# Windowed attention and max-out feed-forward: columns in the order 8 to 255, 0 to 7, 256 to 259

## The chip, the cores and the metric

The kernel runs on one core of a Trainium2 chip. The metric is the time of the device in microseconds. Three runs of the kernel before took 408.97, 409.05 and 409.37 us; the median is 409.05 us. A profile of one execution is read besides: it lists each instruction of the five engines (PE, the matrix engine; DVE, the vector engine; ACT, the scalar engine; POOL and SP, which here mostly issue transfers) and each transfer between memory and the on-chip buffers.

## The reference: what is computed

There are 8 sequences of 4160 positions with 192 features in 8 heads of 24. Each position and head has 7 logits. Their softmax weighs the position itself and the six before it (zeros ahead of a sequence's start). The result goes through a feed-forward layer with two first matrices, of which the larger product is taken element by element.

```python
w = weight_gen - np.max(weight_gen, axis=-1, keepdims=True)
w = np.exp(w)
w = w / (np.sum(w, axis=-1, keepdims=True) + 1e-09)
x_pad = np.concatenate([np.zeros((B, pad, D)), x], axis=1)      # pad = 6
x_unf = x_pad[:, idx, :].reshape(B, S, K, H, group)             # 7 taps
out = np.einsum('bshk,bskhg->bshg', w, x_unf).reshape(B * S, D)
h1 = out @ w1
h2 = out @ w2
return np.maximum(h1, h2) @ w_out                               # 192 -> 1024 -> 192
```

Input and output are 32-bit floats. The kernel computes in bfloat16 behind the softmax.

## The kernel before, in words

**Layout.** The 33280 positions are laid on 128 partitions of 260 consecutive positions each; sixteen partitions hold one sequence. A "column" is one position on every partition. Columns are worked in batches of 16 (the seventeenth has 4). The window of the first six columns of a partition reaches into the end of the partition before; that is the halo. It is masked to zero on the partitions that begin a sequence (`msk`).

**Softmax.** For each batch, ACT takes exp of the logits (`exp_sum`), DVE sums seven taps (`red`), ACT takes the logarithm (`ln`), DVE subtracts it from the logits (`shift`), and ACT takes exp again (`weights`), writing each weight twice in bfloat16. No maximum is subtracted.

**Attention.** DVE multiplies 7 shifted windows of x with the weights (`mul`) and adds them up in three steps (`adds`). In the first two batches (`mul` in pieces of 4 columns) PE does the sum together with the transposition, by matmuls with an identity (`sum_transpose`), and ACT copies the result to `yt`. Later a transposing transfer on SP's queue does it (`transpose`), in units of 8 columns.

**Feed-forward.** Since max(h1, h2) = h1 + relu(h2 - h1), PE multiplies with the difference of the two first matrices (`wd`), ACT takes the relu from the accumulators into `rd`, and PE adds up relu times `wo` and the attention's result times `w10`, the product of the first matrix and `wo`, made once at the start. ACT evicts the output (`evac`), SP stores it. Hidden tiles are worked in groups of two, later three; `hidden` writes each group's order on PE and ACT by hand, and `softmax_steps` and `extra` place the softmax and attention of later batches between them by a table of due times.

**The order around the change.** The program is issued in a written order; every engine works its own list in order. At the start, SP issues the first logits (`load_wg(0, ...)`, L520), the halo in two transfers (L523), the first four x columns (L537), then the rows of the first matrices (`ws`, L541 and L549), the next four x columns, the second halves of these rows, and the second logits. Each of SP's transfers uses one of eight semaphores in turn, so the ninth waits until the first has landed. POOL issues later x and logits. PE runs matmuls without use (`keep_warm`) until the first product is there. `w_diff` builds `wd` on DVE and copies parts across partition halves. At the end `rest_of_results` does the last outputs, and SP waits for all stores.

The lines that carry this are few:

```python
for step in (exp_sum, red, ln, shift):
    for i in range(2):
        step(0, i, 2)
...
first_mul = mul(0, 0)
...
keep_warm(30)
w_diff(0, nc.scalar.copy)
```

Of the kernel before, what the change touches and what calls it, by code (L numbers as in the profile page):

```python
# [9 lines left out]
FP32 = mybir.dt.float32  # L10
# [13 lines left out]
def kernel(  # L24
# [20 lines left out]
    RPB = P // B  # L45
    G = D // H
# [29 lines left out]
    pwg = ctx.enter_context(tc.tile_pool(name="pwg", bufs=4))  # L76
    pxb = ctx.enter_context(tc.tile_pool(name="pxb", bufs=2))
    pe_ = ctx.enter_context(tc.tile_pool(name="pe", bufs=2))
    psm = ctx.enter_context(tc.tile_pool(name="psm", bufs=3))
    pm = ctx.enter_context(tc.tile_pool(name="pm", bufs=1))  # L80
    pen = ctx.enter_context(tc.tile_pool(name="pen", bufs=2))
    py = ctx.enter_context(tc.tile_pool(name="py", bufs=2))
    pyt = ctx.enter_context(tc.tile_pool(name="pyt", bufs=6))
    prd = ctx.enter_context(tc.tile_pool(name="prd", bufs=7))
    first_ps = ctx.enter_context(ExitStack())
# [3 lines left out]
    def later_ps():  # L89

        first_ps.close()
        for k in ("ab", "c", "r"):
            ps[k] = ctx.enter_context(tc.tile_pool(name="pps_" + k, bufs=1, space=bass.MemoryType.PSUM))
# [7 lines left out]
    def load_wg(b, eng):  # L101
        c0, n = BATCHES[b]
        wg_ts[b] = pwg.tile([P, n * WGC], FP32, name="wg_t", tag="wg")
        return eng.dma_start(
            out=wg_ts[b],
            in_=bass.AP(tensor=weight_gen.tensor, offset=c0 * WGC,
                        ap=[[CPP * WGC, P], [1, n * WGC]]),
        )

    def load_x(b, o, n, halo=True):  # L110

        if b not in xb_ts:
            xb_ts[b] = pxb.tile([P, (16 + PAD) * D], BF16, name="xb_t", tag="xb")
        load = nc.gpsimd.dma_start(  # L114
            out=xb_ts[b][:, (PAD + o) * D:(PAD + o + n) * D],
            in_=bass.AP(tensor=x.tensor, offset=(BATCHES[b][0] + o) * D,
                        ap=[[CPP * D, P], [1, n * D]]),
        )
        if b > 0 and o == 0 and halo:
            load_halo(b)  # L120
        return load

    def load_halo(b):

        if b not in xb_ts:
            xb_ts[b] = pxb.tile([P, (16 + PAD) * D], BF16, name="xb_t", tag="xb")
        nc.gpsimd.dma_start(out=xb_ts[b][:, 0:PAD * D],
# [708 lines left out]
```

## Time and profile before

| what | value |
|---|---|
| median of three runs | 409.05 us (408.97 to 409.37) |
| profiled execution, first to last instruction | 408.4 us |
| PE busy | 398.9 us (98%) |
| DVE busy | 371.7 us (91%) |
| ACT busy | 357.1 us (87%) |
| POOL busy | 72.5 us (18%) |
| granted PE clock | 1.000 |
| HBM read, written | 35.96 MB, 25.56 MB |
| first multiply of x and weights on DVE | 9.75 us |
| first hidden matmul on PE | 16.10 us |
| first output matmul on PE | 28.99 us |
| end of DVE's last attention sum | 378.5 us |
| issue of the last stores | 405.38 us |

The profiled execution's own time is its span of 408.4 us, and the runs' median lies 0.65 us above it; the difference is what lies around the first and last instruction. The body is read as a rhythm: PE works three hidden tiles and the outputs that belong to them in about 4.3 us, and ACT's relus and evictions stand in the gaps. A row of the timeline gives the start, the duration, the engine, the line in the code, the operation, what is written and read, and the shapes; in brackets stands the idle time of the engine just before and what ended it.

### The profile page before, as it was taken

What the parts mean: (1) busy time and instruction counts of PE and PEld (TensorE: products, weight loads), DVE (VectorE), ACT (ScalarE), POOL (GpSimd) and SP (SyncE); (2) the same over time, 40 slices, a digit from 0 to 9 for tenths busy, and PEclk for the clock granted to TensorE, in tenths of its full rate; (3) what the DMA queues carried; (4) which work ended last, traced back from release to release, by engine and by line L of the source; (5) the groups of instructions that cost most, each with busy time, mean ns of one, the idle gap of its engine ahead of it and who ended that gap; (6) DMA issues with size and microseconds to landing.
All of it is one profiled execution on the core that took longest, in us unless ns stands there. A gap on an engine that the chain in (4) does not pass through costs nothing.

```text
span 408.4 us, 16153 instructions
## 1 busy us (share of the span) xinstructions
PE 398.9 (98%) x7422; PEld 317.6 (78%) x7422; DVE 371.7 (91%) x216; ACT 357.1 (87%) x424; POOL 72.5 (18%) x101
## 2 busy tenths in 40 slices
PE   7899999999999999999999999999999999999996
PEld 2589989777777777777877777777778777777796
DVE  4999999999999999999999999999999999999000
ACT  6799899999899998898998999998999988988872
POOL 0311012212222112121211122220122220210000
PEclk9999999999999999999999999999999999999999
DMA  8958399767658674976786588478648647654514
GB/s 242 218 125 219 75 186 167 168 165 173 147 113 237 151 167 105 244 201 69 234 203 84 123 248 202 65 243 180 128 109 239 169 68 237 154 127 111 145 55 142
DMA packets 62785, 65.70 MB, mean 161 GB/s; under 512 B 47711, under 2 KB 51679, under 8 KB 62718
## 3 DMA queue, kind: packets, MB, share of 16 engines
q1 hardware_dynamic: 54334, 40.54, 36.7%
q0 software_dynamic: 8240, 24.04, 29.9%
q8 instruction: 58, 0.95, 1.0%
q10 hardware_dynamic: 144, 0.10, 0.1%
q14 instruction: 9, 0.07, 0.1%
HBM read 35.96 MB, written 25.56 MB: 151 GB/s over the span
## 4 chain that ended last, share of the span: by engine, by line
PE 91%; ACT 4%; DMA 3%; issue 1%; SPq 0%; DVE 0%; ACTq 0%
PE op_ps L339 41%; PE hd L299 39%; PE op_ps L351 8%; DMA xs<-in_x_dram 3%; ACT rd_t L309 2%; PE hdp L299 1%; PE yps L248 1%; ACT yt L255 1%; ACT w1t L675 0%; ACT e_t L135 0%; ACT en_t L167 0%; DVE xb_t L620 0%; ACT wd L591 0%; ACT w L668 0%; ACT w1T L633 0%
## 5 line engine op out<-in xcount | busy, mean ns | idle before, releaser
L309 ACT ACTIVATE rd_t<-hd 128x1024 bf16<-128x1024 f32 (+1 forms) x206 | 234.7, 1187 | 27.5 <-PE hd L299 26.3
L339 PE MATMUL op_ps<-wo,rd_t 64*128 64x192 bf16 x4160 | 211.4, 243 | 0.1
L339 PEld LDWEIGHTS <-rd_t 64*128 64x128 bf16 x4160 | 181.7, 94 | 15.7 <-ACTq L372 0.3
L299 PE MATMUL hd<-yt,wd 64*128 64x512 bf16 (+1 forms) x1584 | 188.1, 360 | 0.7 <-issue 0.6
L182 DVE TENSOR_TENSOR m_t<-xb_t,en_t 128x10752 bf16<-128x10752 bf16 (+1 forms) x37 | 187.4, 5070 | 0.2
L299 PEld LDWEIGHTS <-wd 64*128 64x128 bf16 x1776 | 94.5, 94 | 43.2 <-issue 2.8
L224 POOL CAST gate<-yt 128x1 f32<-128x1 bf16 x29 | 37.8, 1305 | 264.3 <-DMA yt<-y_t 264.3
L198 DVE TENSOR_TENSOR m_t<-m_t 128x4608 bf16<-128x4608 bf16 (+1 forms) x30 | 74.1, 2470 | 0.1
L395 ACT COPY o_t<-op_ps 128x384 f32<-128x384 f32 (+1 forms) x99 | 57.3, 589 | 12.8 <-PE op_ps L339 12.8
L351 PE MATMUL op_ps<-w,yt 64*128 64x192 bf16 x780 | 56.0, 243 | 0.4 <-ACT w L668 0.4
L351 PEld LDWEIGHTS <-yt 64*128 64x128 bf16 x780 | 38.6, 94 | 16.7 <-issue 1.3
L204 DVE TENSOR_TENSOR m_t<-m_t 128x3072 bf16<-128x3072 bf16 (+1 forms) x29 | 50.0, 1723 | 0.1
L167 ACT ACTIVATE en_t<-wg_t 128x896 bf16<-128x896 f32 (+2 forms) x45 | 35.8, 821 | 0.0
L207 DVE TENSOR_TENSOR y_t<-m_t 128x1536 bf16<-128x1536 bf16 (+1 forms) x29 | 27.3, 941 | 0.5
L114 POOL DMA_DIRECT2D xb_t<-in_x_dram x33 | 17.6, 534 | 32.0 <-ACT rd_t L309 19.8
L147 DVE TENSOR_REDUCE sum_t<-e_t 128x64 f32<-128x448 f32 (+2 forms) x31 | 19.6, 635 | 3.3 <-ACT e_t L135 3.3
L156 DVE TENSOR_TENSOR wg_t<-wg_t,sum_t 128x280 f32<-128x280 f32 (+5 forms) x46 | 22.0, 481 | 0.0
L135 ACT ACTIVATE e_t<-wg_t 128x896 f32<-128x896 f32 (+2 forms) x18 | 16.1, 901 | 2.6 <-DMA wg_t<-in_weight_gen_dram 2.6
L309 ACT ACTIVATE rd_t<-hdp 128x1024 bf16<-128x1024 f32 x16 | 16.3, 1056 | 0.5 <-PE hdp L299 0.4
L299 PE MATMUL hdp<-yt,wd 64*128 64x256 bf16 x192 | 13.2, 270 | 0.7 <-issue 0.5
L615 PE MATMUL warm<-ident 128*128 128x512 bf16 x38 | 10.7, 449 | 2.6 <-DVE ident L562 2.6
L248 PEld LDWEIGHTS <-m_t 64*128 64x128 bf16 x636 | 10.1, 95 | 2.6 <-DVE m_t L182 2.5
(45 smaller groups left out, 65.9 us busy)
## 6 DMA issues: line engine op xcount, KB each, us to landing
out_dram<-o_t SPq DMA_DIRECT2D x22, 768.0 KB, 4.8
xb_t<-in_x_dram POOLq DMA_DIRECT2D x30, 384.0 KB, 5.2
out_dram<-o_t SPq DMA_DIRECT2D x20, 384.0 KB, 3.1
wg_t<-in_weight_gen_dram POOLq DMA_DIRECT2D x14, 448.0 KB, 5.3
xb_t<-xb_t POOLq DMA_DIRECT2D x16, 288.0 KB, 5.4
wg_t<-in_weight_gen_dram SPq DMA_DIRECT2D x2, 448.0 KB, 4.4
xs<-in_x_dram SPq DMA_DIRECT2D x2, 384.0 KB, 7.2
xb_t<-in_x_dram POOLq DMA_DIRECT2D x3, 192.0 KB, 4.4
```

The lines of the kernel that those rows point to most:

```text
L156: nc.vector.tensor_tensor(out=w_t, in0=w_t, in1=_sub(s_ts[b], hs.start, [[1, hs.stop - hs.start], [0, K]]), op=ALU.subtract)
L167: nc.scalar.activation(out=_sub(en_ts[b], (o * WGC + j * N * K) * 2, [[2 * N, K], [2, N], [1, 2]]), in_=_sub(wg_ts[b], (o * H + j * N) * K ...
L182: return nc.vector.tensor_tensor(out=m_out, in0=x_in, in1=_sub(en_ts[b], o * WGC * 2, [[2, K * n * H], [0, G // 2], [1, 2]]), op=ALU.mult,)
L198: nc.vector.tensor_tensor(out=taps(0, 1, 3), in0=taps(0, 1, 3), in1=taps(3, 1, 3), op=ALU.add)
L204: nc.vector.tensor_tensor(out=taps(0, 2, 2), in0=taps(0, 2, 2), in1=taps(1, 5, 2), op=ALU.add)
L207: nc.vector.tensor_tensor(out=_sub(y_ts[b], o * D, [[64, 2], [P, 3 * w // 2], [1, 64]]), in0=taps(0, 1, 1), in1=taps(2, 1, 1), op=ALU.add,)
L224: nc.gpsimd.tensor_copy(out=gate, in_=yt[:, 0:1])
L299: nc.tensor.matmul(hid_out(t, f, j), lhsT=wd_at(j, s, f // 4, f % 4 * P, P), rhs=_sub(yt_ts[u][half(j), :], (s + j) % 3 * P, [[3 * P, w // ...
L309: relu_of[t0] = nc.scalar.activation(out=rd[:, k * 1024:(k + n) * 1024], in_=hd[:, at:at + n * 1024], func=AF.Relu)
L339: return nc.tensor.matmul(op_out(c), lhsT=rd[half(r), k * 1024 + at:k * 1024 + at + P], rhs=wo[half(r), f * D:(f + 1) * D], start=False, s ...
L351: nc.tensor.matmul(op_out(c + j), lhsT=yt_ts[u][half(j), (3 * i + (s + j) % 3) * P:(3 * i + (s + j) % 3 + 1) * P], rhs=w10[half(j), s * D: ...
L395: nc.scalar.copy(out=_sub(o, c % 24 * D, [[D, len(qs)], [h * D, 2], [1, D]]), in_=_sub(tile_, at + (qs[0] - p) * D, [[D, len(qs)], [512, 2 ...
```

## The change: what it does

- **Order of columns.** The columns are worked in the order 8 to 255, 0 to 7, 256 to 259. `actual` maps the place in the order to the column, for loads and stores. The first batch is now columns 8 to 23; its halo, columns 2 to 7, lies on the same partition and needs no mask. Columns 0 to 7 stand in the batch before the last; their x goes to a tile of its own (`"wrap"`), with a halo from the partition before, loaded on POOL's queue after a memset of one row, and masked by one ACT instruction (`wrap_mask`) shortly before use.
- **Start.** The first logits are loaded in two halves; the second half goes on SP's queue after the weight rows' last 64 rows. The halo and the first four columns come in one transfer each. The second four columns come by POOL's queue, as bfloat16 and behind the first exp. Only the first half of the first softmax is done ahead of the first multiply; the second half stands after the first hidden tiles. `ident` is built ahead of the mask. Two of the three copies of the first `w_diff` move from ACT to DVE. The w1E copy of the second half moves behind the second half's weights. `keep_warm` has 24 and 4 matmuls instead of 30 and 8.
- **Sums.** The sums of the softmax are kept for the whole kernel in two tiles (`s_first`, `s_rest`), and the logarithm is written to a tile of its own.
- **Guard.** At the end (`sums_in_range`) DVE takes the largest and smallest sum, compares them with 1e18 and 1e-18, a transfer brings the 128 results into one row, and one integer is made of them. Every engine loads it into a register. If it is not zero, a loop over 260 columns computes everything again with the maximum subtracted (`with_maximum`); otherwise the engines branch past it.

The diff, cut to its core:

```diff
+    def actual(v):
+        return v + 8 if v < LAST - 8 else v - (LAST - 8) if v < LAST else v
...
+        key, at = (b, o) if c < LAST - 8 else ("wrap", 0) if c < LAST else (NB - 2, 8)
...
+        if "wrap" in xb_ts and t is xb_ts["wrap"]:
+            nc.gpsimd.memset(t[0:1, 0:PAD * D], 0.0)
+            nc.gpsimd.dma_start(
+                out=t[1:P, 0:PAD * D],
+                in_=bass.AP(tensor=x.tensor, offset=(CPP - PAD) * D, ap=[[CPP * D, P - 1], [1, PAD * D]]),
+            )
...
+    def wrap_mask():
+        halo = xb_ts["wrap"][:, 0:PAD * D]
+        nc.scalar.activation(out=halo, in_=halo, func=AF.Copy, scale=msk[:, 0:1])
...
-        load_wg(0, nc.sync)
-        nc.vector.memset(xs[0:1, 0:PAD * D], 0.0)
-        for p0, p1 in ((1, 16), (16, P)):
+        xb_ts[0] = pxb.tile([P, (16 + PAD) * D], BF16, name="xb_t", tag="xb")
+        load_wg(0, nc.sync, 0, 8)
+        for at, c, n in ((0, 2, PAD), (PAD, 8, 4)):
             nc.sync.dma_start(
...
         load_w(0)
-        load_first(4)
+        load_w_rest()
+        load_wg(0, nc.sync, 8, 8)
         load_w(1)
         load_wg(1, nc.sync)
...
-        for step in (exp_sum, red, ln, shift):
-            for i in range(2):
-                step(0, i, 2)
+        first_exp = exp_sum(0, 0, 2)
+        for step in (red, ln, shift):
+            step(0, 0, 2)
...
-        for o in (0, 4, 8, 12):
-            weights(0, o)
+        weights(0, 0)
+        weights(0, 4)
+        for at, n in ((0, PAD), (PAD, 4)):
+            nc.vector.tensor_copy(out=xb_ts[0][:, at * D:(at + n) * D], in_=xs[:, at * D:(at + n) * D])
...
-        keep_warm(30)
-        w_diff(0, nc.scalar.copy)
-        nc.vector.tensor_copy(out=xb_ts[0][:, (PAD + 4) * D:(PAD + 8) * D], in_=xs[:, (PAD + 4) * D:])
+        keep_warm(24)
+        w_diff(0, (nc.scalar.copy, nc.vector.tensor_copy, nc.vector.tensor_copy))
+        behind(first_exp, load_x(0, 4, 4))
         behind(first_mul, load_x(0, 8, 4))
...
-        keep_warm(8)
+        keep_warm(4)
         mul(0, 4)
+        exp_sum(0, 1, 2)
         nc.scalar.copy(out=w1["T"], in_=ws["T", 0])
-        nc.scalar.copy(out=w1["E"][:, HF:F], in_=ws["E", 0][:, HF:F])
...
-        w_diff(1, nc.vector.tensor_copy)
-        sum_transpose(1)
+        w_diff(1, (nc.vector.tensor_copy,) * 3, lambda: red(0, 1, 2))
+        sum_transpose(1, ahead=lambda: ln(0, 1, 2))
+        shift(0, 1, 2)
         red(1)
+        weights(0, 8)
         mul(0, 8)
+        weights(0, 12)
+        nc.scalar.copy(out=w1["E"][:, HF:F], in_=ws["E", 0][:, HF:F])
         hidden(1)
...
+        if s == 4 and b == NB - 3:
+            wrap_mask()
...
+    sums_in_range()
     rest_of_results(OUTS[-1])
+    work.close()
+    again = nc.values_load(odd_any, min_val=0, max_val=1, ...)
+    with tc.If(again != 0, preferred_fallthrough_block=False):
+        with_maximum()
```

and of the new functions at the end:

```python
def sums_in_range():
    for i, (op, test, bound) in enumerate(((ALU.max, ALU.is_gt, SUMS[1]), (ALU.min, ALU.is_lt, SUMS[0]))):
        for j, s_t in enumerate(s_parts):
            at = 2 * i + j
            nc.vector.tensor_reduce(out=odd[:, at:at + 1], in_=s_t, op=op, axis=AX.X)
            nc.vector.tensor_single_scalar(out=odd[:, at + 4:at + 5], in_=odd[:, at:at + 1], scalar=bound, op=test)
    nc.vector.tensor_reduce(out=odd[:, 8:9], in_=odd[:, 4:8], op=ALU.max, axis=AX.X)
    nc.gpsimd.dma_start(out=odd_row, in_=odd[:, 8:9])
    nc.vector.tensor_reduce(out=odd[0:1, 9:10], in_=odd_row, op=ALU.max, axis=AX.X)
    nc.vector.tensor_copy(out=odd_any, in_=odd[0:1, 9:10])
```

## The prediction

> **What bounds the kernel now.** I read the busy line and the chain on the page first, then the waits of TensorE (PE), then the timeline of the first 35 us and of the last 10. The page, parts 1 and 4:
>
> ```profile
> PE 398.9 (98%) x7422; PEld 317.6 (78%) x7422; DVE 371.7 (91%) x216; ACT 357.1 (87%) x424; POOL 72.5 (18%) x101
> ...
> PE 91%; ACT 4%; DMA 3%; issue 1%; SPq 0%; DVE 0%; ACTq 0%
> ```
>
> The body is PE's: the table of 10 us windows gives PE 10.00 of 10 from 60 us to 400 us. So only what moves PE's start, what stalls it, and what follows its last matmul can move the end. PE's waits show the start:
>
> ```profile
> PE warm L615 <- DVE ident L562: 2.6, 1, 2.6
> PE yps L248 <- DVE m_t L182: 1.3, 1, 1.3
> ...
> PE op_ps L351 <- ACT w L668: 0.4, 1, 0.4
> ```
>
> The third is the last real wait: the first output matmul (28.99 us) waits for ScalarE's (ACT's) copies of w10. From there PE runs on. The timeline shows what leads there:
>
> ```profile
> 9.08 0.56 DVE L574 CAST xb_t<-xs 128x768 bf16<-128x768 f32 x1 [1.40 <-DMA xs<-in_x_dram]
> 9.75 2.96 DVE L182 TENSOR_TENSOR m_t<-xb_t,en_t 128x5376 bf16<-128x5376 bf16 x1
> ...
> 12.77 1.40 PE L248 MATMUL yps<-ident,m_t 64*128 64x64 bf16 x84 [1.29 <-DVE m_t L182]
> ...
> 13.34 0.62 ACT L586 COPY wd<-wd 64x512 bf16<-64x512 bf16 x1 [2.48 <-DVE wd L584]
> ...
> 15.26 0.80 ACT L255 CAST yt<-yps 128x768 bf16<-128x768 f32 x1
> ...
> 28.30 0.64 ACT L668 CAST w<-pw 64x192 bf16<-64x192 f32 x2
> ...
> 28.99 0.42 PE L351 MATMUL op_ps<-w,yt 64*128 64x192 bf16 x6 [0.35 <-ACT w L668]
> ```
>
> VectorE (DVE) idles 1.40 us until the first x columns land at 9.06, multiplies from 9.75 (call this start X), PE transposes, and from 15.26 ACT works without a gap to 28.94. That is the start's critical path: the x transfer, the first multiply, then ACT.
>
> **Part 1: when the first multiply starts.** The transfers ahead of it shrink from 448+67.5+504+384 = 1403 KB to 224+576+384 = 1184 KB. 219 KB at the first slice's 242 GB/s are 0.9 us: landing 8.15, if the rest stays. Two things do not. In the packet records one 3072-byte packet of this transfer took 1.84 us (median 0.17), and 14 of its 16 shares had landed by 7.4: without such a straggler the new landing would be near 6.4. And the second x columns, formerly SyncE's (SP's) after the weight rows, are now issued by POOL right after the first exp. That exp can end near 4.2 (half a logit load, 0.52 for the half exp); POOL's first packet came 1.37 after its issue at 13.02, so packets flow from 5.6, beside the end of the transfer we wait for. The same 192 KB piece needed 0.97 us alone (16.45 to 17.42 in the middle shares), so SP's is delayed by up to 0.97; I take 0.7, what of it lies before the landing. Bounds: 7.05 (no straggler) and 8.85 (the same one); no row tells which, so I take the middle, 8.0. With 0.58 for the cast and 0.11 to the next start, X = 8.7 (7.75 to 9.55) instead of 9.75. The cast of the six halo columns (1152 elements, 0.84 by L574's rate), which replaces the masked copies L568 and L570, runs while the later transfer flows: free; without that cover 0.84.
>
> The Trainium skill, "DMA: Bandwidth & Descriptors", section "Queues, rings and completion order", has each DMA engine take turns between queues, a packet of some nine or more rows at a time. By that rule POOL's eight rows pass in one turn, and the landing would be 8.3 instead of 8.0. The trace has both queues moving at once from 14.4 to 16.4 us, but does not show the turns.
>
> **Part 2: from X to the w10 copies.** Before, ACT's first `yt` copy waited behind three `wd` copies and began at X+5.51. Now two of those are DVE's, and the copy starts when PE is done: 2.96 + 0.05 + 1.40 + 0.05 = X+4.46. A gain of 1.05. But the half of the first softmax that ran under the transfer wait now stands in ACT's and DVE's gapless stretch. DVE from X, by start-to-start times: multiply 2.88, two differences 0.60 and 0.75, two copies 0.60, multiply 2.88, difference 0.72, half reduction 0.53, three copies 0.87, half shift 0.57: done at X+10.40. The cast L620 (0.72) is gone. ACT: `yt` 0.69, half exp 0.45, copy 0.52, relu 0.92, exp 0.84, relu 0.90 end at X+8.85; the half ln waits for the half reduction (X+9.0); the second `yt` ends at X+9.98; the four weight exps wait for the shift: X+10.43. Then 4 x 0.30, the w1E copy 0.52, two relus 1.82, ln 0.19, two relus 1.81, w1t 1.37, two exps 0.60, `yt` 0.68, relu 0.91, w10 copies 1.13: end X+20.66. Before: 28.94 = X+19.19. So the stretch is 1.47 longer and break-even is at X = 8.28. With X = 8.7, PE's body starts 0.42 later; bounds -0.53 and +1.27. DVE's own path (its third multiply ends at X+14.31 instead of X+13.37) gives -0.1 and is covered by ACT's. The T rows of the weights pass the same DMA engines: 384 KB more ahead and 219 less put them near 11 to 12.7 against the need at X+3.48 = 12.2: even; a lateness there adds one to one.
>
> The early `ident` (the 1.02 us memset L521 leaves DVE) and the 24+4 instead of 30+8 warm matmuls change only filler: PE's gap before the transposes grows from 1.3 to about 2.5 us. If that gap cost PE its clock (the first warm matmuls stand 0.43 apart, later ones 0.21), transposes and first hidden tiles (2.9 us) would double; the page grants full clock in all slices, and I cost it at nothing.
>
> **Part 3: the body.** Sums go to long-lived tiles and ln to a new one: same instructions, no new wait. Storing columns elsewhere costs nothing; the stores are the same size. Two logit loads instead of one for batch 15: 0.55 of POOL, which idles 9 us before its next gate. New is the mask of the late halo: POOL memset and a 127-row transfer, then one ACT instruction of 1152 elements in group 78, about 352 us:
>
> ```profile
> 351.68 0.26 ACT L151 ACTIVATE sum_t<-sum_t 128x32 f32<-128x32 f32 x1
> 351.86 1.02 ACT L309 ACTIVATE rd_t<-hd 128x1024 bf16<-128x1024 f32 x1
> 353.18 0.80 ACT L395 COPY o_t<-op_ps 128x768 f32<-128x768 f32 x1 [0.30 <-PE op_ps L339]
> 354.53 2.86 ACT L309 ACTIVATE rd_t<-hd 128x1024 bf16<-128x1024 f32 x3 [0.56 <-PE hd L299]
> ```
>
> By L570 (864 elements, 1.02) it takes 1.35. It stands between the short ln and the relu; the relu slips by 1.35, ACT's idle 0.30 takes some, the eviction is 1.05 late. PE needs that PSUM tile after two hidden tiles, 0.45 after the eviction ended: a stall of 0.6. The halo transfer, issued near 347 behind POOL's load (345.38) and memset, lands in 3 to 5 us, in time or up to 1 late in the same place. Low bound 0 (if the eviction's real slack is larger), high 1.5; I take 0.6.
>
> **Part 4: the end.** The check of the sums is 11 DVE instructions and a POOL transfer after DVE's last sum at 378.5: four reductions over 384 or 1696 values (1.08 for 896 read, L147) make about 5 us, the transfer 4; done by 390, under PE's tail. If it were not, every engine's end would wait. After the last store each engine now loads a register from SBUF, compares, and branches over the rarely run block; SP also passes four more waits.
>
> ```profile
> 404.87 0.48 ACT L383 COPY o_last<-op_ps 128x384 f32<-128x384 f32 x1
> 405.38 0.34 SPq L386 DMA_DIRECT2D out_dram<-o_last  x1
> ```
>
> SP's last issue ends at 405.72, its 13 closing waits take 0.065 each, yet it finishes them at 407.49, as the last store lands at 407.4: 0.9 slack. Added: four waits 0.26, branch steps 0.16, and the register load. No row shows one: at least a wait (0.06), at most a round trip like the last store's (1.8). I take 1.0, as it moves one word but must go to SBUF and back. 1.42 - 0.9 = 0.5 late. The jump may need instructions not fetched yet: the page's instruction queue moved 58 packets of 16 KB, median 0.98 us, at most 1.76. Zero or one such, I take 0.3 for it: tail +0.8 (0 to 2.9).
>
> **The sum.** 0.4 + 0.6 + 0.8 = +1.8 us. The profiled execution spans 408.4 us, 0.65 below the median 409.05 of the runs shown; the span becomes 410.2, the run 410.85.
>
> **The rivals.**
> A, faster: the straggler and POOL's competition both stay away from the first x transfer, X falls to 7.4 (then DVE's own shift and casts bound it), and PE starts 0.9 early; it decides if X < 7.5 while mask and branch hide. Time 408.1. For it: 14 of 16 shares landed by 7.4 already before. Against it: POOL's packets from 5.6, and the end's extra steps stand on a path with 0.9 slack.
> B, no change: X = 7.75, start -0.5, mask 0.3 and tail 0.5: 409.35. The regrouping only pays for the guard.
> C, a late start: the same straggler, X = 9.55 or the T rows late by as much, start +1.3, rest as forecast: 411.75.
> D, the branch's fetch falls on SP or ACT in full (0.98 instead of 0.3) and the register load is a full 1.8: tail 0.7 + 0.8 above my +0.8, so +2.3, 412.35. For it: the queue's 0.98 per packet; against it: PE and DVE reach the branch early, and the jump is some 60 instructions. The Trainium skill, "Runtime: NRT & Kernel Launch", section "Instruction fetch mechanics", states that a taken branch whose target lies outside the fetched window waits for a fetch; the trace of before has no such branch to agree with.
>
> **How the numbers follow.** My forecast has 0.32, A 0.12, B 0.22, C 0.20, D 0.14. C and the forecast differ in X alone. Less than 0.2% (0.8 us) is about what a measurement of this kernel can tell from no change. Faster holds A: 0.12. Same holds B: 0.22. Slower holds the rest: 0.66. The range reaches to A and leaves out what lies beyond it and C together with D (413.25): 408.1 to 412.9. The forecast's own range is 410.0 to 411.7.
>
> **What the changed profile would show.** Part 1: the first multiply's start, near 8.7, and whether POOL's first x packets lie beside SP's. Part 2: the w10 copies ending at X+20.7, the wait for them still PE's last, with four exps and a half exp and ln inside ACT's gapless stretch. Part 3: a wait of PE near 352 with the mask instruction before it. Part 4: more time between the last store's issue and the end, 2.7 us now (405.72 to 408.4), 3.5 expected. I am wrong if the w10 copies end before 28.6, if PE loses nothing at the mask, or if the end still takes 2.7 us.

## The result, and the profile after

The changed kernel took 414.56 us (median of 4 runs, 413.00 to 416.69) beside 409.21 us for the kernel before: a ratio of 1.0119, 95% interval 1.0080 to 1.0158. It is slower, as forecast, by 5 us instead of 1.8, and outside the range of 408.1 to 412.9. The profiled execution took 413.0 us and spans 411.1.

Parts 1 and 4 of the page after:

```profile
PE 397.3 (97%) x7412; PEld 316.5 (77%) x7412; DVE 377.5 (92%) x227; ACT 356.5 (87%) x422; POOL 78.0 (19%) x105
...
PE 53%; DVE 34%; ACT 4%; issue 4%; DMA 3%; SPq 1%; POOL 0%; DVEq 0%; ACTq 0%
```

PE is busy as long as before (397.3 against 398.9), so the time went into waits. In the chain DVE's share rose from 0% to 34%: from the mask the chain goes back through POOL to DVE, which works without a pause of 0.2 us or more from about 203 to 344 us. The list of waits (who waited for whom; us in total, times, longest) names the place, ACT's wait and PE's:

```profile
ACT xb_t L150 <- issue: 2.7, 1, 2.7
...
PE yps L284 <- DVE m_t L218: 2.4, 2, 1.6
...
PE op_ps L388 <- ACT o_t L432: 3.1, 1, 3.1
...
PE op_ps L388 <- ACT w L703: 0.4, 1, 0.4
```

A wait of 3.1 us has come into the body, at 353 us, where PE had none. The wait for w10 is as before (0.4). The timeline around the new wait:

```profile
344.62 0.54 POOL L133 DMA_DIRECT2D xb_t<-in_x_dram  x1 [0.31 <-DVE s_rest L180]
...
345.14 1.05 POOL L141 MEMSET xb_t<- 1x1152 bf16 x1
...
346.14 0.55 POOL L142 DMA_DIRECT2D xb_t<-in_x_dram  x1
...
350.65 0.27 ACT L186 ACTIVATE ln_t<-s_rest 128x32 f32<-128x32 f32 x1
...
353.59 1.25 ACT L150 ACTIVATE xb_t<-xb_t,msk 128x1152 bf16<-128x1152 bf16 x1 [2.67 <-issue]
354.75 1.00 ACT L346 ACTIVATE rd_t<-hd 128x1024 bf16<-128x1024 f32 x1
...
355.65 0.79 ACT L432 COPY o_t<-op_ps 128x768 f32<-128x768 f32 x1
...
356.49 0.42 PE L388 MATMUL op_ps<-w,yt 64*128 64x192 bf16 x6 [3.07 <-ACT o_t L432]
```

Read it from below: PE waits 3.07 us for the eviction that ends at 356.44; the eviction stands on ACT behind a relu, the relu behind the mask (L150), and ACT idles 2.67 us before the mask. The page calls that wait "issue", since it finds no releaser among the engines: it is the halo transfer L142, issued at 346.14, whose sixteen shares report landing at 350.63 to 353.51. The chain, in order of time (start, length, what), says the same with its pieces from DVE's sum (L180) to the mask:

```profile
344.26 0.19 DVE s_rest L180
344.45 0.16 issue
344.62 0.54 POOL xb_t L133
345.15 0.99 POOL xb_t L141
346.14 4.78 DMA xb_t<-in_x_dram
350.92 2.67 issue
353.59 0.07 ACT xb_t L150
```

POOL's loads wait for DVE there, so the halo's issue hangs on DVE's pace, and the load and the memset stand ahead of it. PE's lead over the kernel before goes from 1.0 us ahead to 2.2 behind in this one place: its hidden tiles begin at 351.94 against 352.96 before, the matmuls behind the wait at 356.49 against 354.26.

The start, from the same timeline:

```profile
6.82 0.56 DVE L604 CAST xb_t<-xs 128x768 bf16<-128x768 f32 x1 [0.47 <-DMA xs<-in_x_dram]
7.48 2.96 DVE L218 TENSOR_TENSOR m_t<-xb_t,en_t 128x5376 bf16<-128x5376 bf16 x1
...
11.25 0.69 DVE L617 TENSOR_TENSOR wd<-ws1T,ws0T 128x512 bf16<-128x512 f32 x1 [0.21 <-DMA ws1T<-in_moe_w_dram]
...
12.87 2.96 DVE L218 TENSOR_TENSOR m_t<-xb_t,en_t 128x5376 bf16<-128x5376 bf16 x1
...
28.12 0.64 ACT L703 CAST w<-pw 64x192 bf16<-64x192 f32 x2
...
28.81 0.42 PE L388 MATMUL op_ps<-w,yt 64*128 64x192 bf16 x6 [0.42 <-ACT w L703]
```

The first multiply starts 2.3 us earlier than before (7.48 against 9.75), yet the w10 copies end only 0.18 earlier (28.76 against 28.94). The chain's first pieces tell what stands there now:

```profile
4.98 6.25 DMA ws1T<-in_moe_w_dram
11.23 0.02 issue
11.25 0.70 DVE wd L617
```

Before, the chain began with two x loads, the second landing at 13.96 ahead of the cast L620 and the second multiply:

```profile
13.98 0.62 DVE L620 CAST xb_t<-xs 128x768 bf16<-128x768 f32 x1
14.70 2.96 DVE L182 TENSOR_TENSOR m_t<-xb_t,en_t 128x5376 bf16<-128x5376 bf16 x1
```

Now it begins with the last of the weight rows, landing at 11.23; the second multiply stands behind their difference and its copies, at 12.87. From the second multiply to the end of w10 it takes 15.89 us, against 14.24 before. And the end:

```profile
407.05 0.48 ACT L420 COPY o_last<-op_ps 128x384 f32<-128x384 f32 x1
407.56 0.35 SPq L423 DMA_DIRECT2D out_dram<-o_last  x1
```

SP's last issue ends at 407.90 and the span at 411.12: 3.22 us, against 2.67 before.

The same places in twelve of the twenty profiles, the experiments below among them. X is the start of the first multiply; "T rows" the landing of the last 64 weight rows; "body" the time from the end of the w10 copies to the end of SP's last issue; "halo" the time from the issue of the late halo's transfer to its last share; all in us.

| kernel | X | T rows | w10 end | halo | PE stall at the mask | body | end | span |
|---|---|---|---|---|---|---|---|---|
| before | 9.75 | 12.98 | 28.94 | - | - | 376.8 | 2.67 | 408.4 |
| before, again | 9.82 | 13.03 | 29.03 | - | - | 376.4 | 2.66 | 408.1 |
| changed | 7.48 | 11.23 | 28.76 | 7.37 | 3.07 | 379.1 | 3.22 | 411.1 |
| changed, again (e7) | 7.67 | 12.25 | 29.59 | 7.01 | 2.74 | 380.4 | 3.24 | 413.2 |
| changed, third (e16) | 7.82 | 11.98 | 29.41 | 7.29 | 3.27 | 378.6 | 3.23 | 411.2 |
| mask late (e1) | 8.56 | 12.69 | 30.19 | 6.83 | 0 | 376.1 | 3.24 | 409.5 |
| mask late, again (e18) | 8.36 | 12.58 | 30.00 | 5.70 | 0 | 376.2 | 3.21 | 409.5 |
| no guard (e2) | 8.03 | 12.08 | 29.64 | 5.85 | 1.57 | 379.6 | 2.75 | 412.0 |
| no guard, again (e17) | 7.46 | 11.93 | 29.21 | 5.99 | 1.68 | 377.8 | 2.81 | 409.9 |
| small block (e4) | 8.93 | 12.96 | 30.61 | 5.81 | 1.53 | 377.6 | 2.81 | 411.0 |
| late, no guard (e6) | 7.82 | 11.99 | 29.49 | 5.93 | 0 | 376.1 | 2.85 | 408.5 |
| late, no guard, again (e15) | 7.73 | 11.90 | 29.30 | 7.42 | 0 | 375.9 | 2.72 | 407.9 |

Every run of either kernel lies 1.7 to 2.0 us above its span. Without a long stall at the mask the body is 376.4 and 376.8 in the two profiles of the kernel before and 375.4 to 376.3 in twelve of changed kernels, so a few tenths between two rows mean nothing. But for the stall the changed kernels lose nothing in the body; it is some 0.6 shorter, and no run shows why. The long body of e2 holds another gap of PE, 1.5 us at 64 us.

### The profile page after: what moved, and what is told of

It reads as the page before. It is cut to its first block, busy times and chain, and to the rows that moved or that the text cites. A ratio compares the mean times of both kernels' runs of the same rounds, so it can differ in the third digit from the quotient of the medians.

```text
span 411.1 us, 16181 instructions
## 1 busy us (share of the span) xinstructions
PE 397.3 (97%) x7412; PEld 316.5 (77%) x7412; DVE 377.5 (92%) x227; ACT 356.5 (87%) x422; POOL 78.0 (19%) x105
## 4 chain that ended last, share of the span: by engine, by line
PE 53%; DVE 34%; ACT 4%; issue 4%; DMA 3%; SPq 1%; POOL 0%; DVEq 0%; ACTq 0%
PE op_ps L376 24%; PE hd L336 22%; DVE m_t L218 17%; DVE m_t L234 7%; DVE m_t L240 5%; PE op_ps L388 5%; ACT rd_t L346 2%; DVE s_rest L180 2%; DMA ws1T<-in_moe_w_dram 2%; DVE y_t L243 1%; PE hdp L336 1%; DVE wg_t L191 1%; DMA xb_t<-in_x_dram 1%; PE yps L284 1%; ACT en_t L202 1%
## 5 line engine op out<-in xcount | busy, mean ns | idle before, releaser
L260 POOL CAST gate<-yt 128x1 f32<-128x1 bf16 x29 | 40.4, 1392 | 258.9 <-DMA yt<-y_t 258.9
L191 DVE TENSOR_TENSOR wg_t<-wg_t,ln_t 128x280 f32<-128x280 f32 (+5 forms) x46 | 22.1, 481 | 0.4 <-ACT ln_t L186 0.3
L180 DVE TENSOR_REDUCE s_rest<-e_t 128x64 f32<-128x448 f32 (+2 forms) x27 | 16.3, 603 | 0.4 <-ACT e_t L162 0.4
L284 PE MATMUL yps<-ident,m_t 64*128 64x64 bf16 x636 | 10.7, 190 | 2.4 <-DVE m_t L218 2.4
```

The costliest lines, as they stand in the source:

```text
L191: nc.vector.tensor_tensor(out=w_t, in0=w_t, in1=_sub(s_ts[b], hs.start, [[1, hs.stop - hs.start], [0, K]]), op=ALU.subtract)
L260: nc.gpsimd.tensor_copy(out=gate, in_=yt[:, 0:1])
```

## The experiments

Ratios are to the kernel before on the same chip, with their 95% intervals.

**First set: is it the mask's wait, and what does the guard cost?** The kernel before stood at 410.15 us.

The mask three groups later:

```diff
-        if s == 4 and b == NB - 3:
+        if s == 7 and b == NB - 3:
             wrap_mask()
```

> One edit to the changed kernel: the mask instruction on ACT stands one group of three tiles later (at place 7 of batch 14 instead of 4). Theory W (the mask stands on ACT's list before its halo has landed at 353.5 us, and everything behind it on ACT waits): the landing is unchanged, the mask starts without a wait near 358, PE's stall of 3.07 falls under 0.6, the profiled span falls from 411.1 to about 408.5, and the spread of the runs over several us goes with it. Rival I (the instruction's own 1.25 us on ACT is what costs, wherever it stands): the stall moves with it and the time stays within 1 us of the changed kernel.

Measured: 410.86 us, ratio 1.0007 (0.9986 to 1.0029). ACT's timeline has the mask without any idle time before it:

```profile
357.85 0.50 ACT L432 COPY o_t<-op_ps 128x384 f32<-128x384 f32 x1
...
358.21 1.29 ACT L150 ACTIVATE xb_t<-xb_t,msk 128x1152 bf16<-128x1152 bf16 x1
...
359.37 1.90 ACT L346 ACTIVATE rd_t<-hd 128x2048 bf16<-128x2048 f32 x1
```

The instruction takes as long (1.29) and PE loses nothing. Nearly all of the loss went with the mask's place; e5 below parts the wait for the transfer from the instruction. The span fell to 409.5, not to 408.5, as this start was late (w10 at 30.19), and the runs spread over 1.8 us instead of 3.7.

The mask taken out (the halo of columns 0 to 5 is not set to zero where a sequence starts):

```diff
-        if s == 4 and b == NB - 3:
-            wrap_mask()
```

> The changed kernel without the mask instruction, so the halo of columns 0 to 5 is not zeroed on the partitions that begin a sequence. Theory W: PE's stall at 353 us vanishes whole, span 411.1 - 3.2 = 407.9, runs near 409.7 with a spread under 0.5. If a stall of 0.5 us or more stays at the same place, something else in the order of ACT there is slow (rival O).

Measured: 410.96 us, ratio 1.0018 (0.9999 to 1.0038), no gap of PE in the body after 50 us. The mask late and no mask are the same within the intervals: placed late, its work is free. The stall is gone whole, as theory W asked. The time stands 1.3 above its 409.7, of which 0.9 is the higher time of the kernel before on this chip, and the runs spread over 1.6 us, not under 0.5.

The guard taken out:

```diff
-    sums_in_range()
...
-    again = nc.values_load(odd_any, min_val=0, max_val=1, ...)
-    with tc.If(again != 0, preferred_fallthrough_block=False):
-        with_maximum()
```

> The changed kernel without the check of the sums, the register loads and the branch (sums are still kept in their two tiles; a case of sums out of range is not handled, as in the kernel before). Theory T (the branch costs on the path after the last store's issue and also outside the span): from the last issue to the end 2.7 us instead of 3.2, and the time outside the span falls from 1.9 to about 0.65 us; in all 1.8 us off, the stall at the mask and its spread stay. Rival F (what lies outside the span grows by something else in the change, as the start): the time outside the span stays at 1.9.

Measured: 412.88 us, ratio 1.0071 (1.0042 to 1.0100). From SP's last issue the end took 2.75 us instead of 3.22. The stall at the mask is there without the guard (1.57). The time outside the span stays 1.8, so the guard costs nothing there; that was rival F.

The guard kept, but its block cut to one memset (the second computation is left out):

```diff
     with tc.If(again != 0, preferred_fallthrough_block=False):
-        with_maximum()
+        nc.vector.memset(odd, 0.0)
```

> The changed kernel with check, register loads and branch, but in the rarely run block stands one memset instead of the loop over 260 columns. Theory T1 (register load and branch cost, not the size of what they jump over): last issue to end 3.2 us and 1.9 us outside the span as in the changed kernel. Rival T2 (the block's size: loop, registers, more instructions to load): the time outside the span falls to 0.65 to 1.2 us and the step from the branch to SP's closing waits, 0.47 us, falls to 0.1.

Measured: 412.68 us, ratio 1.0070 (1.0039 to 1.0102); end 2.81. Over all profiles the end takes 3.21 to 3.24 with the whole guard and 2.72 to 2.86 without it, so the guard costs 0.4 to 0.5 there, and 2.81 with the small block lies among those without: what costs is the jump past the long block. The register load (0.52 on SP), the comparison (0.06) and the branch lie under the last store's landing. In the changed kernel's records SP passes four more waits ahead of the branch and pauses 0.47 us between the branch (ended 409.01) and its first closing wait (409.48); with the small block the four waits are not there and the pause is 0.15.

**Second set: what is left when both are gone?** The kernel before stood at 409.38 us.

The changed kernel again, unedited:

> The changed kernel itself, on the chip of this set, so that the other runs have it beside them. Theory W+S (mask stall of 1.5 to 3 us, plus a start and an end that are 0.5 to 1 us worse): ratio to before 1.007 to 1.012. With the two earlier runs that hold the mask at its place and leave out the guard or its block (1.007 each), the full guard is worth 0 to 2 us.

Measured: 415.14 us, ratio 1.0137 (1.0090 to 1.0183), above what was expected. The profiled execution shows a second price of the stall, in the table of windows around its end (columns: window and length, then busy time of PE, PEld, DVE, ACT, POOL with instructions, the granted PE clock, DMA share and GB/s):

```profile
353.92:357.33 3.41, 0.67 (x15) 0.41 (x11) 3.41 (x3) 3.32 (x4) 1.18 (x2) 1.00 0.94 304
357.33:360.74 3.41, 3.41 (x39) 2.70 (x36) 3.41 (x5) 2.28 (x3) 0.00 (x0) 0.50 0.47 62
360.74:364.15 3.41, 3.41 (x65) 2.70 (x62) 3.41 (x2) 2.38 (x3) 0.00 (x0) 1.00 0.41 77
```

PE worked 0.67 us of one stretch, and in the next its clock is granted at half: 39 matmuls are counted instead of 65. That is up to 1.7 us more, and this body is 1.3 longer than the first profile's although its stall is 0.3 shorter. The first profile did not have it. The changed kernel's first four timed executions with mean clocks 0.999, 0.995, 0.990 and 0.987 spanned 411.1, 412.6, 412.9 and 414.8.

The halo's transfer ahead of the x columns:

```diff
     def load_x(b, o, n, halo=True):
         t, at = x_at(b, o)
+        if "wrap" in xb_ts and t is xb_ts["wrap"]:
+            nc.gpsimd.dma_start(out=t[1:P, 0:PAD * D], ...)
         load = nc.gpsimd.dma_start(...)
...
             nc.gpsimd.memset(t[0:1, 0:PAD * D], 0.0)
-            nc.gpsimd.dma_start(out=t[1:P, 0:PAD * D], ...)
```

> The changed kernel with the halo's transfer issued ahead of the batch's x on POOL's queue, and the memset behind both; the mask stays at its place. Theory W (the wait is for the landing of that transfer): the issue comes 1.5 us earlier (344.6 instead of 346.1), the landing as much, the mask waits about 1.2 us instead of 2.7, PE's stall falls from 3.07 to about 1.5. Rival P (a transfer's straggling share sets the landing, whatever the issue): the stall stays between 1.5 and 3 us.

Measured: 410.93 us, ratio 1.0045 (1.0027 to 1.0062).

```profile
344.80 0.55 POOL L134 DMA_DIRECT2D xb_t<-in_x_dram  x1 [0.44 <-DVE s_rest L181]
345.34 0.56 POOL L138 DMA_DIRECT2D xb_t<-in_x_dram  x1
345.87 1.05 POOL L146 MEMSET xb_t<- 1x1152 bf16 x1
...
350.91 1.28 ACT L151 ACTIVATE xb_t<-xb_t,msk 128x1152 bf16<-128x1152 bf16 x1
...
353.84 0.42 PE L389 MATMUL op_ps<-w,yt 64*128 64x192 bf16 x6 [0.29 <-ACT o_t L433]
```

The halo landed 4.34 us after its issue, in time; the mask stands in its first place without waiting, and PE loses 0.29. That is what the instruction alone costs there. The time stands 1.0 us above e6 below, on the same chip and without guard, of which this and the guard's 0.45 at the end make 0.7. Theory W had asked for a landing only 1.5 us earlier and a stall of 1.5; it came 4.4 us earlier, as the transfer itself was shorter ahead of the load (4.34 instead of 7.37, and 5.02 in e11, which sends it first too).

The mask late and no guard (both edits above):

> The changed kernel with the mask one group later and without the guard (sums out of range are then not handled, as before). What is left of the change is the order of columns and the start. Theory S (the start's earlier multiply is used up by ACT's longer stretch, body start +0.5 on average; less by small PE waits): span 0 to 0.5 us above before's, ratio 0.999 to 1.002. Rival G (the start is a real gain hidden so far by mask and guard): ratio 0.996 or less.

Measured: 409.90 us, ratio 1.0014 (0.9995 to 1.0034). With mask and guard gone the kernel is still not faster: the start brings nothing.

The same, with a copy of weight rows taken from ACT:

```diff
-        nc.scalar.copy(out=w1["E"][:, HF:F], in_=ws["E", 0][:, HF:F])
+        nc.gpsimd.tensor_copy(out=w1["E"][:, HF:F], in_=ws["E", 0][:, HF:F])
```

> As the run before, with the 0.60 us copy of the second half of w1E moved from ACT to POOL. Theory S (ACT's gapless stretch to the w10 copies sets PE's body): the w10 copies end 0.5 us earlier after the first multiply, X+21.0 instead of X+21.5, and the whole falls by 0.5. Rival V (DVE's third multiply sets it): nothing moves.

Measured: 410.70 us, ratio 1.0034 (1.0020 to 1.0048). Taking 0.6 us from ACT's stretch did not shorten it: w10 ended 17.98 us after the T rows, later than in the fourteen others that leave the first transfers as changed (17.26 to 17.65). But the run tells little of ACT's work. Beside POOL's cast (18.31 to 18.94) DVE's copy L621 took 1.05 us, against 0.29 in e6; PE waited 1.01 for that copy, and ACT 1.12 for DVE's shift behind it, against 0.44 in e6. What was taken from ACT came back through DVE.

**Third set: is it the clock at the start?** The kernel before stood at 409.82 us, and once more by itself:

> The kernel before once more, for a second look at it and as the measure of how far two profiled executions of one kernel lie apart. Ratio 1.000 within 0.002. Its profiled span should lie near 407.6 if the first profiled execution (408.4) was a slow one, and its first multiply at or before 9.75: near 8 if the straggling share of the first x transfer was chance, 9.7 again if it belongs to the order of the transfers.

Measured: 409.62 us, ratio 0.9993 (0.9967 to 1.0019). Its x transfer landed at 9.13 and X was 9.82: what the prediction took for one packet's bad luck happened in both profiles of this kernel. In the changed kernels X lay between 7.23 and 8.93 in all but one; in that one (e14) the transfer landed at 9.13, too.

More matmuls without use, with the mask late and no guard:

```diff
-        keep_warm(24)
+        keep_warm(32)
```

> The changed kernel with the mask three groups later, without the guard, and with 32 instead of 24 matmuls without use ahead of the first transposition. The same kernel with 24 stood 0.45 us above the kernel before (ratio 1.0014). Theory C (the clock): PE's idle time before the first transposition sends it to half clock for 3.41 us in a good third of the executions, and that costs what of the transposition and the first hidden tiles ACT then waits for; with 8 more (1.7 us) the idle time falls from 1.6 to 2.9 us to at most 1.2, no half-clock stretch stands in the start, the share of runs with a mean clock under 0.997 falls from 0.3 to under 0.1, and the ratio to 1.0000 to 1.0010. Rival N: the start is set by ACT, which needs its 21.6 us from the first multiply to the end of w10 whatever PE's clock is; the stretch goes but the ratio stays at 1.0014 within 0.0010, and in an execution with an early first multiply the extra matmuls even delay the transposition.

Measured: 410.81 us, ratio 1.0028 (1.0012 to 1.0044). In the late-mask kernel's start a half-clock stretch stands behind PE's idle time of 2.86 us (e1):

```profile
8.58:11.99 3.41, 0.55 (x29) 0.42 (x30) 3.41 (x2) 0.62 (x1) 0.16 (x1) 1.00 1.09 284
11.99:15.40 3.41, 3.41 (x72) 1.96 (x64) 2.72 (x5) 2.30 (x4) 1.80 (x3) 0.50 1.11 291
```

With 32 matmuls the share of executions with a mean clock under 0.997 fell from 0.30 (e6; 0.58 in the later e15) to 0.08, as theory C says, but no time came of it. In its profile the transposition waited for the extra matmuls, 0.9 us behind the multiply that feeds it, and w10 still ended 17.29 after the T rows. Rival N fits better than theory C: the stretch went and nothing was won, though 1.0028 lies above N's band (up to 1.0024), too. Over all profiles of changed kernels w10 ended 17.3 to 17.7 us after the T rows in the starts with a half-clock stretch, and as much after them in those without (e8 and e14 apart).

All of it together (the halo first, the mask late, 32 matmuls, guard kept):

> The changed kernel whole, guard included, with what the runs so far pointed to: the late halo transferred ahead of the x columns, the mask three groups later, and 32 matmuls without use at the start. The prices so far: start 0.45 us, guard's end 0.5, mask 0. Sum: 0.9 to 1.0 above the kernel before, ratio 1.0023, as good as the late mask alone gave (1.0007 to 1.0018). By theory C 0.2 to 0.4 less than that, ratio 1.0015. Whether it beats the kernel before: no theory says so; it would need the first multiply before 7.2 us, and DVE's own work ahead of it does not allow that.

Measured: 411.02 us, ratio 1.0036 (1.0020 to 1.0053), above the expectation and no better than the mask's place alone.

**Fourth set: what sets the start?** The kernel before stood at 409.92 us. All but the last are edits of the kernel with late mask and no guard, whose control is

> The control: the changed kernel with the mask three groups later and without the guard, as run before (ratio 1.0014). First multiply 7.8, T rows landed near 12.0, w10 copies end near 29.5.

Measured: 410.31 us, ratio 1.0004 (0.9980 to 1.0027).

The T rows later on SP's queue:

```diff
-        load_w_rest()
         load_wg(0, nc.sync, 8, 8)
+        load_w_rest()
```

> As the control, but the second half of the first logits goes ahead of the T rows on SP's queue instead of behind them. The first multiply stays near 7.8. Theory T: the T rows land 0.5 to 0.8 later, near 12.6, and the w10 copies end as much later, near 30.1; time 0.5 to 0.8 above the control (ratio 1.0030). Theory A: the w10 copies stay 21.6 behind the first multiply, or come earlier, as the half exp has its logits sooner; time as the control.

Measured: 410.77 us, ratio 1.0014 (0.9993 to 1.0034). DVE's timeline:

```profile
7.91 2.96 DVE L218 TENSOR_TENSOR m_t<-xb_t,en_t 128x5376 bf16<-128x5376 bf16 x1
...
12.98 0.69 DVE L617 TENSOR_TENSOR wd<-ws1T,ws0T 128x512 bf16<-128x512 f32 x1 [1.51 <-DMA ws1T<-in_moe_w_dram]
...
14.34 2.96 DVE L218 TENSOR_TENSOR m_t<-xb_t,en_t 128x5376 bf16<-128x5376 bf16 x1
```

The T rows landed at 12.90 and DVE waited 1.51 us for them; w10 ended at 30.24, which is 22.3 after the first multiply but 17.34 after the rows. By the trace the rows set the start here. The time is 0.46 above the control's in the medians, nearly the least that theory T asked (0.5), though the intervals overlap.

The other direction, POOL's second x columns later:

```diff
-        behind(first_exp, load_x(0, 4, 4))
+        behind(first_shift, load_x(0, 4, 4))     # first_shift: what shift(0, 0, 2) returns
```

> As the control, but POOL's second x columns wait for DVE's first difference instead of the first exp: their issue moves from 4.3 to about 5.65. Theory T (the T rows set the start): these columns share the transfer engines with the T rows; with 1.3 us less of that at half rate, the T rows land 0.4 to 0.7 earlier, near 11.4, the w10 copies end 17.3 to 17.65 behind them, near 28.9, and the time falls by 0.4 to 0.6 against the control (ratio to the kernel before 1.0000 to 1.0005). Theory A (ACT's stretch behind the first multiply): w10 ends 21.6 after the first multiply as ever, the time stays within 0.2 of the control. A third, the columns themselves come late: they land after 12.9 and the second multiply waits for them.

Measured: 410.36 us, ratio 1.0000 (0.9978 to 1.0022). This did not do what it was for. In its profile all transfers were late (X 8.47), the T rows landed at 12.42, 3.95 behind X instead of 4.17, and the time is the control's. The same edit in the whole kernel, guard kept and mask late:

> The changed kernel whole, guard included, with the mask three groups later and POOL's second x columns behind DVE's first difference. With the mask alone moved it stood at 1.0007 to 1.0018. Theory T: 0.4 to 0.6 us less, ratio 0.9995 to 1.0008, level with the kernel before. Theory A: ratio 1.0010 to 1.0020.

Measured: 410.40 us, ratio 1.0012 (0.9986 to 1.0038); it tells nothing apart.

**Fifth set: mask and guard on one chip.** The kernel before stood at 410.15 us.

> The changed kernel, as the measure for the next two. Ratio 1.0120 to 1.0137 if the loss is the kernel's own; PE stall at the mask 2.7 to 3.1 us, in most executions a half-clock stretch behind it.

Measured: 414.01 us, ratio 1.0104 (1.0077 to 1.0131), stall 3.27. The profile has no half-clock stretch behind it; four of the six executions have mean clocks of 0.990 to 0.995.

> The changed kernel without the guard (no check of the sums, no register load, no branch). Theory W (the mask's wait is the loss, the guard costs its 0.5 at the end): 0.3 to 0.7 us below the changed kernel on the same chip, ratio 1.0105 to 1.0125, stall at the mask as there. Rival V (the guard makes the mask's stall longer, in a way the trace has not shown): 2 us or more below it, ratio near 1.0071 again, stall 1.5 us.

Measured: 412.45 us, ratio 1.0096 (1.0058 to 1.0134), stall 1.68. By the ratio the guard costs 0.3 us, by the medians 1.6; the seven runs spread over 5.5 us, so this pair alone decides nothing. The stall was short again without the guard, as rival V says. What tells against V is the halo's transfer in all sixteen profiles that issue it in its old place: with the guard it took 7.37, 7.01, 7.29, 6.83, 5.70 and 7.21 us, with the small block 5.81, without the guard or the mask 5.85, 5.99, 5.93, 7.16, 6.96, 7.42, 5.72, 7.18 and 6.52. Both kinds have both lengths, so it looks to be the execution that decides, not the guard; with the mask in its first place alone, the three profiles with the whole guard (7.0 to 7.4) and the three with none or the small block (5.8 to 6.0) do not overlap.

> The changed kernel with the mask three groups later, guard included. Theory W: 4 to 5 us below the changed kernel, ratio 1.0007 to 1.0025, no PE stall near 353. Rival V gives the same for this one; should it stand at 1.006 or more, something other than the mask's wait and the guard's end costs on this chip.

Measured: 411.00 us, ratio 1.0018 (1.0003 to 1.0033). On one chip the mask's place alone is worth 3.5 us (1.0104 - 1.0018 of 410), or 3.0 by the medians, where theory W had 4 to 5.

No version beat the kernel before. The best that keeps the guard, the late mask, stands at 1.0007 and 1.0018.

## Why the prediction was right or wrong

**Right: what bounds it, and the sign.** PE's body was the bound, and the change lost by a stall there and by the end, with a start that did not pay. The chance of 0.66 stood on the right side.

**Wrong: part 3, the landing of the late halo.** The step that failed is "lands in 3 to 5 us, in time or up to 1 late", and with it the stall of 0.6 with an upper bound of 1.5. It landed 5.7 to 7.4 us after its issue. In the six profiles with the mask and the halo's transfer in their first places the stall follows that landing one to one, at landing minus 4.3 (3.07, 2.74, 3.27, 1.57, 1.68, 1.53 against 3.1, 2.7, 3.0, 1.6, 1.7, 1.5). The instruction by itself was sized about right: 1.25 instead of 1.35, and 0.29 of stall instead of 0.6 where the halo is in time. The rows for the right size were on the page of before, in the list of issues with their median time to landing:

```profile
xb_t<-in_x_dram POOLq DMA_DIRECT2D x30, 384.0 KB, 5.2
...
xb_t<-xb_t POOLq DMA_DIRECT2D x16, 288.0 KB, 5.4
```

With 5.4 from 347 the halo lands at 352.4, behind the 351.86 at which the mask was to start. The median alone would have given a stall near 1.1, and a bound from the slowest of these loads more. The load and the memset ahead of it on POOL's queue were in the 347, but not weighed as a place where time could be lost: sent first, ahead of them, the halo landed 4.34 us after its issue and was in time.

**Left out: what a stall of 3 us does next.** The prediction asked of PE's clock only at the start. In e7 a half-clock stretch of 3.41 us followed the stall; three of the changed kernel's first four executions and seven of its ten later ones have mean clocks of 0.987 to 0.995 (one such stretch takes 0.004 off the mean), part of which can be from the start. These ten took 413.3 to 416.7 us, the four others, at 0.997 or more, 412.8 to 413.1, 2.1 less on the mean; in kernels without the stall the same split is worth 0.8 us in e1, 0.6 in e18 and e15, 0.1 in e6. The Trainium skill, "TensorE: Matmul & The Clock Gate", section "Part 1: The HAM clock gate (the "warmup" mystery)", states that the clock drops to half after an idle window of about 3.4 us, and that the window runs freely. The length of the stretch agrees, and so does the free running; a window that is idle as a whole does not. Of the idle times that led to a stretch here most were shorter, from 1.82 us on, and others of 2.24, 3.07 and 3.27 us led to none.

The clock records show what tells them apart. In every one of the twenty profiles the changes of the granted clock lie whole multiples of 3.41 us from one another (16 in e7, 116 in e1, from the one half-clock stretch to the next). Cut the time from 7 to 400 us along that grid: nine pieces are followed by a half-clock stretch, and in them PE was busy for 0 to 1.59 us of 3.41; no other piece of any profile has PE busy for less than 1.54. So what tells is how the wait falls on the grid, more than its length. The 2.74 us of e7 lay whole in one piece (0.67 busy). The 3.07 and 3.27 of the other two profiles were cut by a border into pieces with 1.54 and 2.21, and 1.71 and 1.85, busy. The grid lies differently to the program in each execution, so for who plans a kernel a wait of 2 to 3 us has this price by chance.

**Part 1: right in direction, late by 0.9.** X was 7.2 to 8.9, median 7.8 over the fifteen profiles that leave the first transfers as changed, against 8.7 (7.75 to 9.55). The term that failed is the 0.7 for POOL's competition: POOL's first x packets came at 7.2 to 7.6 us, some 3 us behind their issue instead of 1.37, and in ten of the fifteen the transfer they were to delay had landed by then. It landed at 6.5 to 8.2, median 7.1, near the bound without a straggler (7.05).

**Part 2: the stretch right, its start wrong.** The w10 copies ended at 28.8 to 30.6, median 29.5, so PE's body began 0.5 later than before; 0.42 was forecast. The first `yt` copy began at X+4.46 as worked out in eight of them, and at up to X+5.48 in the others, where the transposition came later or ran longer. From the second multiply to the end of w10 it took 15.9 to 16.0 us (16.1 in e8), against 14.24 and 14.26 before; the prediction's own rows give 15.83 (20.66 - 4.83): the half exp, ln and the exps inside it cost what they were said to. But the second multiply did not follow X. It came at X+5.4 to X+6.0 instead of X+4.83, since DVE waited 0.2 to 1.0 us for the T rows and in some profiles took 0.3 longer for the copies behind them, so that it is only some 1.2 earlier than before, not 2. From the rows to the end of w10 it took 17.3 to 17.65 in fourteen of the fifteen (e8 is the other), whatever X was. The sentence "a lateness there adds one to one" was right, "even" was not: with X almost a us earlier than taken, the rows are needed earlier too, and do not land earlier. So the total agreed by luck: X was taken 0.9 too late, and the second multiply's lateness behind X was left out, about as much the other way. That the rows set it is what the traces show, with e13 for the later landing; that an earlier one would win the time was tried (e12) and not shown. Whether ACT's work by itself sets the rest of the stretch, as the prediction has it, stays open, since in e8 DVE was slowed as well.

**The warm matmuls** "cost at nothing": in the executions with a half-clock stretch the transposition took longer, as the prediction said it would (2.11 instead of 1.40 in e1). It cost nothing that shows up to w10, as the T rows were later still.

**Part 4: +0.8 forecast, +0.55 measured** in the profile. The register load is 0.52 instead of 1.0; the pause behind the far branch 0.47 instead of 0.3. SP's closing waits in the trace of before are ten, not 13, so the slack was nearer 1.1 than 0.9. The guard's own work on DVE was done at 386 with a wait of 2.2 us for its transfer, all under PE's tail, as costed.

**The sum.** The 0.65 us between span and median was no constant of the runs: every run lies 1.7 to 2.0 above its span, and the profiled execution of before was itself one of the longer ones (about 410.2). It did no harm, as only the +1.8 was carried over. By medians the loss of 5.35 comes out as 0.5 for the start, 0.55 for the end, some 2.6 for the stall at the median landing of 6.9, 0.6 less for the rest of the body, and what remains, about 2.3, for half-clock stretches. This last term is what is left over; it was seen behind the stall in one profile only, but the 2.1 us between executions with and without a stretch fit it.

**The rivals.** A's condition on X held in the profile (7.48), and the start still came only 0.18 early, as the T rows stood behind it. Rival C named these rows as a cause of a late start. D's far branch is there at 0.47, and smaller than D.

## What to carry to other kernels

Cost a new transfer by the landing times that the page lists for its own queue and size in the loaded body, and add what is issued ahead of it on that queue; then ask whether its first reader stands in order ahead of work that the bound engine needs. When an early wait is shortened, look for the next transfer that lands at a fixed time, since it can take the gain. And a stall of two or three us on PE is to be costed with the half-clock stretch that may follow: half of 3.41 us, with a chance.

## What the runs showed of the hardware that was not expected

The late halo's data were there 0.5 to 2.0 us before the transfer counted as landed. In the packet records its last data packet ended 5.1 to 5.6 us after the issue in the six profiles with a stall, but the last of its sixteen shares was reported at 5.8 to 7.4. The list of issues and queues for 346 to 354 us of the changed kernel shows what ran beside it:

```profile
q1 hardware_dynamic: 1212, 0.69, 60.6%
q0 software_dynamic: 288, 0.69, 50.5%
q8 instruction: 1, 0.02, 0.8%
...
xb_t<-in_x_dram POOLq DMA_DIRECT2D x1, 285.8 KB, 7.4
yt<-y_t SPq DMA_TRANSPOSE x1, 5.0
```

A transposing transfer with packets of 256 bytes was issued on SP's queue 3.75 us after the halo. In the slice from 5 to 6 us after the halo's issue, in which the last of its data came, 485 packets of SP's queue took 50 us of the sixteen engines' time, some 0.1 each, against 0.02 in the slice from 7 to 8. The Trainium skill, "DMA: Bandwidth & Descriptors", section "Queues, rings and completion order", states that the write which reports a share is ordered behind all earlier writes of its DMA engine, across queues. That would make the halo wait for the transposing packets, and the numbers agree with it, as do e5 and e11, where the halo was issued 5 us ahead of the transposing transfer and landed after 4.34 and 5.02. But there the halo was also ahead of the load, and no run moved the transposing transfer alone, so this is argued and not shown. Why some executions report at 5.8 and others at 7.4 stays open: the same slice holds 449 packets with 43 us in e4, which reported at 5.81.

The branch past a long block costs SP a pause of 0.47 us, against 0.15 with a block of one instruction, and the end takes 0.4 less with the short one, though neither block is run.
